# Attention of the second and third token block in chunks of 64 tokens, all eight heads at once, on quarters of the array

## The chip, the cores and the metric

The kernel runs on one core of a Trainium2 chip. Its time is the device time of one execution in microseconds (us). The engines are TensorE (PE, with its weight loads as PEld), VectorE (DVE), ScalarE (ACT), GpSimd (POOL) and SyncE (SP), which issues the DMAs.

## What is computed

Decayed linear attention over 2 x 8 heads, 768 tokens and a head dimension of 64, then two MLPs (512 to 2048 to 512) over the 1536 tokens. The attention goes over blocks of tokens with a state of 64 x 64 for each head:

```python
intra = np.einsum('bhic,bhjc->bhij', qb, kb) * Dmask[None]
intra = np.einsum('bhij,bhjd->bhid', intra, vb)
inter = np.einsum('bhid,bhde->bhie', qb * lam_pow[None], kv_state)
out[:, :, sl] = intra + inter
kv_state = lam_block[None, :, None, None] * kv_state + np.einsum('bhsd,bhse->bhde', kb_dec, vb)
...
x = _moe_ref(x=x, **moe_kwargs)
return _moe2_ref(x=x, **moe2_kwargs)
```

The length of a chunk is free, since any split of the tokens gives the same result.

## The kernel before, in words

The tokens are in three blocks of 512 (T). The first MLP runs block by block, each in 16 steps f (128 of the 2048 hidden features), then the second MLP over all blocks. A step is 12 matmuls into `h` (`mlp_h`) and, two steps later, 12 into `y` (`mlp_y`), each with 512 columns (`mm3`, lines 313 to 316: three single-pass matmuls stand for one of full precision, with high and low parts of weights and inputs). VectorE and ScalarE also turn the raw weights into these parts (`make_w1_ops`, lines 113 to 129) and apply the nonlinearity (lines 336 to 343).

Attention works in chunks of 128 tokens (C) and in two groups g of four heads, so each block has eight pairs (chunk, group). The eight of the first block run at the start (lines 494 to 525). Those of the second and third block are woven into the MLP steps of the block before: `att_visit` (line 537) runs at steps 0, 2, 4, ... 14 and 15 of the first block's MLP and at 2, 4, ... 14 and 15 of the second's, 17 visits (line 587). A visit issues the scores of the next pair (`att_s`, line 198) and the rest of the pair before (`att_av`): the values (line 238), the part from the state (line 244, not for the first chunk of a batch) and the update of the state (line 251, not for the last). Each is four matmuls in float32. The scores take 64 rows of the array and all its columns; two heads lie in the two row halves and write two PSUM banks. The other three take all rows and 64 columns, so two heads lie in the two column halves. All but the update stream 128 columns; the update streams 64.

After the visit ScalarE scales the state (line 256), copies the output (line 269) and scales the keys (line 208), GpSimd scales the queries (line 217), and VectorE adds the update to the state in two halves (line 284) and multiplies the scores by the mask in two halves (line 223). All orders are written out by hand, that of each engine and that of the DMA queue on SP. A pair's load is two DMAs of 256 KB in rows of 2 KB (line 173), with two buffers for each.

## Time and profile before

| what | us |
|---|---|
| median of three runs (594.11 to 595.8) | 595.7 |
| the profiled execution | 594.52 |
| its span, first to last instruction | 592.7 |
| TensorE busy in the span | 579.5 |
| VectorE busy in the span | 474.6 |

Busy time counts records, and matmuls overlap, so a busy TensorE can still run with more or less in it. A row of the timeline gives the start, the length and the number of instructions that were merged; the number of partitions x elements follows. `pa_s` are the PSUM tiles of the visits, `pa` and `att` those of the first block's attention. A matmul in float32 shows as two records, one of the MLP as one.

### The profile page before, as it was taken

The page shows a single profiled execution, that of the slowest core. Times are in us where ns is not written, and L with a number is a line of the kernel's source. Part 1 is how long each engine was busy: PE and PEld are TensorE (multiplying, and loading weights), DVE is VectorE, ACT ScalarE, POOL GpSimd, SP SyncE. Part 2 cuts the span into 40 slices and gives each one's busy share as a digit, 9 for nine tenths or more (in the row PEclk, how much of TensorE's full clock was granted, in tenths as well). Part 3 has the DMA queues.
Part 4 walks back from the last instruction along what each step waited for, and adds up shares of the span by engine and source line. Part 5 has one row for each costly group of instructions (what it writes and reads, how often), then busy time and mean ns, then how long its engine had stood idle before and what let it go on. Part 6 is the DMA issues. An engine that isn't in the chain of part 4 may idle for free.

```text
span 592.7 us, 8157 instructions
## 1 busy us (share of the span) xinstructions
PE 579.5 (98%) x3038; PEld 475.8 (80%) x3038; DVE 474.6 (80%) x772; ACT 352.4 (59%) x647; POOL 21.8 (4%) x37
## 2 busy tenths in 40 slices
PE   8878999999999999999999999999999999999997
PEld 7766888888888887888888888888888888888885
DVE  5999998975577653487798999988799888798882
ACT  3464456565434434555558887666777666866762
POOL 5200000000000000000000000000000000000000
PEclk9988999999999999999999999999999999999999
DMA  8954552556367532334443430000210000100001
GB/s 297 401 191 153 203 194 88 186 190 195 107 196 229 162 125 71 143 126 173 134 156 92 131 116 0 1 0 1 103 40 1 1 0 1 71 1 0 2 0 72
DMA packets 25961, 64.49 MB, mean 109 GB/s; under 512 B 2882, under 2 KB 2882, under 8 KB 25922
## 3 DMA queue, kind: packets, MB, share of 16 engines
q1 hardware_dynamic: 25922, 63.98, 31.8%
q8 instruction: 24, 0.39, 0.3%
q14 instruction: 15, 0.12, 0.1%
HBM read 53.48 MB, written 10.49 MB: 108 GB/s over the span
## 4 chain that ended last, share of the span: by engine, by line
PE 94%; DVE 5%; issue 1%; ACT 0%; DVEq 0%
PE y L314 15%; PE y L315 14%; PE y L316 14%; PE h L316 14%; PE h L315 14%; PE h L314 14%; PE pa_s L198 2%; PE pa_s L238 1%; DVE w L129 1%; PE pa L198 1%; DVE w L76 1%; PE pa_s L244 1%; DVE w L73 1%; PE pa L238 1%; DVE w L70 1%; PE pa L462 1%
## 5 line engine op out<-in xcount | busy, mean ns | idle before, releaser
L314 PE MATMUL h<-xlo,w 128*128 128x512 f32 x384 | 151.0, 393 | 5.6 <-DVE b L338 3.0
L316 PE MATMUL h<-xhi,w 128*128 128x512 f32 x384 | 150.9, 393 | 1.1 <-DVE w L129 1.1
L314 PE MATMUL y<-glo,w 128*128 128x512 f32 x384 | 151.3, 394 | 0.0
L315 PE MATMUL h<-xhi,w 128*128 128x512 f32 x384 | 150.6, 392 | 0.0
L316 PE MATMUL y<-ghi,w 128*128 128x512 f32 x384 | 149.6, 389 | 0.0
L315 PE MATMUL y<-ghi,w 128*128 128x512 f32 x384 | 149.5, 389 | 0.0
L314 PEld LDWEIGHTS h<-xlo,w 128*128 128x128 f32 x384 | 72.8, 190 | 21.8 <-DVE b L338 3.4
L316 PEld LDWEIGHTS h<-xhi,w 128*128 128x128 f32 x384 | 72.9, 190 | 17.2 <-DVE w L129 2.0
L314 PEld LDWEIGHTS y<-glo,w 128*128 128x128 f32 x384 | 72.0, 188 | 16.1 <-issue 0.7
L315 PEld LDWEIGHTS h<-xhi,w 128*128 128x128 f32 x384 | 72.8, 189 | 15.0
L316 PEld LDWEIGHTS y<-ghi,w 128*128 128x128 f32 x384 | 72.1, 188 | 15.2
L315 PEld LDWEIGHTS y<-ghi,w 128*128 128x128 f32 x384 | 72.1, 188 | 14.5
L349 ACT ACTIVATE a<-h,babs 128x512 f32<-128x512 f32 x48 | 33.0, 687 | 61.9 <-PE h L316 61.8
L340 ACT ACTIVATE ghi<-b 128x512 fp32r<-128x512 f32 x48 | 30.0, 628 | 43.7 <-DVE b L338 43.6
L336 ACT ACTIVATE a<-h 128x512 f32<-128x512 f32 x48 | 28.4, 592 | 39.9 <-PE h L316 39.7
L353 DVE SCALAR_TENSOR_TENSOR b<-b,babs,a 128x512 f32<-128x512 f32 x48 | 36.0, 750 | 19.6 <-ACT b L350 19.6
L341 DVE TENSOR_TENSOR glo<-b,ghi 128x512 fp32r<-128x512 f32 x48 | 33.5, 699 | 16.1 <-ACT ghi L340 13.9
L338 DVE SCALAR_TENSOR_TENSOR b<-a,h 128x512 f32<-128x512 f32 x48 | 32.7, 681 | 10.3 <-ACT a L337 7.0
L128 ACT ACTIVATE w<-w 128x512 fp32r<-128x512 f32 (+1 forms) x23 | 18.4, 800 | 36.7 <-DVE w L76 34.2
L351 ACT ACTIVATE p<-h,cab 128x512 f32<-128x512 f32 x48 | 37.6, 784 | 0.0
L355 ACT ACTIVATE a<-b,one 128x512 f32<-128x512 f32 x48 | 34.9, 728 | 3.4 <-DVE b L353 2.9
L357 DVE SCALAR_TENSOR_TENSOR p<-p,cab,h 128x512 f32<-128x512 f32 x48 | 35.8, 745 | 1.2
(75 smaller groups left out, 699.0 us busy)
## 6 DMA issues: line engine op xcount, KB each, us to landing
raw<-w_in SPq DMA_DIRECT2D x46, 512.0 KB, 3.8
raw<-w_in SPq DMA_DIRECT2D x9, 1024.0 KB, 4.9
att<-qkv_in SPq DMA_DIRECT2D x16, 256.0 KB, 5.4
qk<-qkv_in SPq DMA_DIRECT2D x16, 256.0 KB, 4.6
kv<-qkv_in SPq DMA_DIRECT2D x16, 256.0 KB, 3.3
w2d<-wp SPq DMA_DIRECT2D x16, 256.0 KB, 4.2
w<-w2d SPq DMA_DIRECT2D x16, 256.0 KB, 2.7
x2d<-o SPq DMA_DIRECT2D x12, 256.0 KB, 2.2
```

What stands on the lines that cost most here:

```text
L314: nc.tensor.matmul(acc, lhsT=wh, rhs=xl, start=first, stop=False)
L315: nc.tensor.matmul(acc, lhsT=wh, rhs=xh, start=False, stop=False)
L316: nc.tensor.matmul(acc, lhsT=wl, rhs=xh, start=False, stop=last)
L336: lambda: nc.scalar.activation(out=a, in_=h, func=AF.Relu, scale=-1.0),
L338: lambda: nc.vector.scalar_tensor_tensor(out=b, in0=a, scalar=-1.0, in1=h, op0=ALU.add, op1=ALU.max),
L340: lambda: nc.scalar.activation(out=ghi, in_=b, func=AF.Copy),
L341: lambda: nc.vector.tensor_tensor(out=glo, in0=b, in1=ghi.bitcast(F32), op=ALU.subtract)]
L349: nc.scalar.activation(out=a, in_=h, func=AF.Abs, scale=babs[:, 0:1])
L351: nc.scalar.activation(out=p, in_=h, func=AF.Identity, scale=cab[:, 3:4], bias=cab[:, 2:3])
L353: nc.vector.scalar_tensor_tensor(out=b, in0=b, scalar=babs[:, 1:2], in1=a, op0=ALU.mult, op1=ALU.add)
L355: nc.scalar.activation(out=a, in_=b, func=AF.Ln, bias=one[:, 0:1])
L357: nc.vector.scalar_tensor_tensor(out=p, in0=p, scalar=cab[:, 1:2], in1=h, op0=ALU.add, op1=ALU.mult)
```

## The change

In the second and third block a chunk is 64 tokens and holds all eight heads, which makes 16 chunks in place of 16 pairs. There are again 17 visits, at steps 2, 4, ... 12, 13, 14, 15 and at 2, 4, ... 14, 15. All four kinds of matmul now have 64 rows, 64 columns of the array and 64 columns streamed. There are eight of each kind in a visit. The scores of the next chunk are issued in turn with the values of the last one, and the updates with the state parts, so that four following matmuls address the four quarters of the array. The mask of two heads is put one below the other by a GpSimd copy. VectorE multiplies the scores in one instruction and adds the state in one; ScalarE scales the state in four. The first block keeps its chunks of 128, but its last chunk adds the old state to the update on TensorE, by an identity, and leaves it in the new layout. A chunk's load is eight DMAs of 64 KB in pieces of 256 bytes, with three buffers. The first is issued behind the weights of step 3, two more at steps 0 and 1, and the others behind the visits from step 4 on.

```diff
     def att_kq(c, g):
         qk, kv, kq = group[c, g][0], att_tile(c, g, 1), att_tile(c, g, 3)
-        if c % CB < CB - 1:
-            for a in range(2):
-                for h2 in range(2):
-                    r, h = slice(h2 * D, (h2 + 1) * D), 4 * g + 2 * a + h2
-                    if c >= NC:
-                        nc.scalar.activation(out=kq[:, 0, a, r], in_=kv[:, a, 0, r], func=AF.Copy,
-                                             scale=dmask[:, h, C - 1:C])
-            if c < NC:
-                nc.gpsimd.tensor_tensor(
-                    out=kq[:, 0].rearrange("p a (h d) -> p a h d", h=2),
-                    in0=kv[:, :, 0].rearrange("p a (h d) -> p a h d", h=2),
-                    in1=dmask[:, 4 * g:4 * g + 4, C - 1:C].rearrange("p (a h) i -> p a h i", h=2)
-                    .to_broadcast([P, 2, 2, D]), op=ALU.mult)
-        if c % CB:
+        nc.gpsimd.tensor_tensor(
+            out=kq[:, 0].rearrange("p a (h d) -> p a h d", h=2),
+            in0=kv[:, :, 0].rearrange("p a (h d) -> p a h d", h=2),
+            in1=dmask[:, 4 * g:4 * g + 4, C - 1:C].rearrange("p (a h) i -> p a h i", h=2)
+            .to_broadcast([P, 2, 2, D]), op=ALU.mult)
+        if c:
             nc.gpsimd.tensor_tensor(out=kq[:, 1], in0=qk[:, :, 0], in1=qpow[:, 2 * g:2 * g + 2],
...
@@ -244,47 +224,140 @@
                     nc.tensor.matmul(ps[0][r, 2 + a], lhsT=state[:, 2 * g + a, h2],
                                      rhs=kq[:, 1, a], start=False, stop=True,
                                      skip_group_check=True)
-        if not last:
+        for a in range(2):
+            for h2 in range(2):
+                r = slice(h2 * D, (h2 + 1) * D)
+                ro = slice((1 - h2) * D, (2 - h2) * D) if last else r
+                nc.tensor.matmul(pu[ro, a], lhsT=kq[:, 0, a, r], rhs=kv[:, a, 1, r],
+                                 start=a == 0 or not last, stop=not last, skip_group_check=True)
...
+        if last:
+            low()
             for a in range(2):
                 for h2 in range(2):
-                    r = slice(h2 * D, (h2 + 1) * D)
...
+                    ro = slice((1 - h2) * D, (2 - h2) * D)
+                    nc.tensor.matmul(pu[ro, a], lhsT=ident, rhs=state[:, 2 * g + a, h2],
+                                     start=False, stop=True, skip_group_check=True)
+            nc.scalar.activation(out=state[:, gs_, 0], in_=pu, func=AF.Copy)
+            return
...
+    CS = D
+    KB = CB * C // CS
+    ROWS = [slice(0, D), slice(D, P)]
+    chunk = {}
+    aa_tiles = []
+    def sm_load(k):
+        c, b = k // 2, k % 2
+        qk = qq.tile([P, NP, 2, CS], F32, tag="qk", name=f"qk{k}")
+        kv = qq.tile([P, NP, 2, D], F32, tag="kv", name=f"kv{k}")
+        chunk[k] = {"qk": qk, "kv": kv}
+        row = 4 * P
+        feat, nat = qkv[c, 0, 0], qkv[c, 0, 1]
+        step = C + (CS if b == 0 else -CS)
+        for rho, r in enumerate(ROWS):
+            for g in range(NP // 2):
+                nc.sync.dma_start(out=qk[r, 2 * g:2 * g + 2], in_=bass.AP(
+                    feat.tensor, feat.offset + (g * 2 * P + (1 - rho) * D) * row + b * CS,
+                    [[row, D], [2 * C, 2], [step, 2], [1, CS]]))
+                nc.sync.dma_start(out=kv[r, 2 * g:2 * g + 2], in_=bass.AP(
+                    nat.tensor, nat.offset + (g * 2 * P + (1 - b) * CS) * row + (1 - rho) * D,
+                    [[row, CS], [P, 4], [1, D]]))
+    def sm_products(n, d):
+        if not aa_tiles:
+            aa_tiles.extend(pa.tile([P, T], F32, tag=f"pa{i}", name=f"aa{i}")
+                            .rearrange("p (x m i) -> p x m i", x=2, m=NP) for i in range(2))
+            for r in ROWS:
+                nc.tensor.matmul(aa_tiles[1][r, 1], lhsT=pick[r], rhs=mask64[r, :, 1:CS + 1],
+                                 start=True, stop=True, skip_group_check=True)
+            nc.scalar.activation(out=qpow[:, :, 0:CS], in_=aa_tiles[1][:, 1], func=AF.Copy)
+        pn, pd = chunk.get(n), chunk.get(d)
+        for m in range(NP):
+            if pn:
+                for r in ROWS:
+                    nc.tensor.matmul(aa_tiles[0][r, 0, m], lhsT=pn["qk"][r, m, 1],
+                                     rhs=pn["qk"][r, m, 0], start=True, stop=True,
+                                     skip_group_check=True)
+            if pd:
+                for i, r in enumerate(ROWS):
+                    nc.tensor.matmul(aa_tiles[1][ROWS[1 - i], 0, m], lhsT=pd["kv"][r, m, 1],
+                                     rhs=pd["s"][r, m], start=m == 0, stop=d % KB == 0,
+                                     skip_group_check=True)
+        for m in range(NP):
+            if pd and d % KB < KB - 1:
+                for r in ROWS:
+                    nc.tensor.matmul(aa_tiles[0][r, 1, m], lhsT=pd["kv"][r, m, 0],
+                                     rhs=pd["kv"][r, m, 1], start=True, stop=True,
+                                     skip_group_check=True)
+            if pd and d % KB:
+                for i, r in enumerate(ROWS):
+                    nc.tensor.matmul(aa_tiles[1][ROWS[1 - i], 0, m], lhsT=state[r, m, 0],
+                                     rhs=pd["qk"][r, m, 0], start=False, stop=True,
+                                     skip_group_check=True)
+    def sm_decay(n):
+        qk, kv = chunk[n]["qk"], chunk[n]["kv"]
+        if n % KB < KB - 1:
+            for m in range(NP):
+                nc.scalar.activation(out=kv[:, m, 0], in_=kv[:, m, 0], func=AF.Copy,
+                                     scale=mask64[:, m, CS - 1:CS])
+        if n % KB:
+            nc.gpsimd.tensor_tensor(out=qk[:, :, 0], in0=qk[:, :, 0], in1=qpow[:, :, 0:CS],
+                                    op=ALU.mult)
+    def sm_mask(n):
+        b = chunk[n]
+        b["s"] = s = ap_.tile([P, NP, CS], F32, tag="s", name=f"s{n}")
+        nc.vector.tensor_tensor(out=s, in0=aa_tiles[0][:, 0], in1=mask64[:, :, 0:CS], op=ALU.mult)
+    def sm_out(d):
+        t, js = d * CS // T, slice(d * CS % T, d * CS % T + CS)
+        if t not in xraw:
+            xraw[t] = xr.tile([P, NP, T], F32, tag="xr", name=f"xr{t}")
+        first, last = d % KB == 0, d % KB == KB - 1
+        if not (first or last):
+            for m in range(NP):
+                nc.scalar.activation(out=state[:, m, 0], in_=state[:, m, 0], func=AF.Copy,
+                                     scale=qpow[:, m, CS - 1:CS])
+        nc.scalar.activation(out=xraw[t][:, :, js], in_=aa_tiles[1][:, 0], func=AF.Copy)
+        if first:
+            nc.scalar.activation(out=state[:, :, 0], in_=aa_tiles[0][:, 1], func=AF.Copy)
+        elif not last:
+            nc.vector.tensor_tensor(out=state[:, :, 0], in0=aa_tiles[0][:, 1],
+                                    in1=state[:, :, 0], op=ALU.add)
...
-        qq = actx.enter_context(tc.tile_pool(name="qq", bufs=2))
+        qq = actx.enter_context(tc.tile_pool(name="qq", bufs=3))
...
+        diag = ws.tile([P, DM], F32, tag="w", name="diag")[:, 0:C + 1]
+        tabs = ac.tile([P, 2, D], F32, name="tabs")
+        pick, ident = tabs[:, 0], tabs[:, 1]
...
+        for last in (D - 1, P - 1):
+            nc.gpsimd.affine_select(out=pick, in_=pick, pattern=[[0, D]], base=-last,
+                                    channel_multiplier=1, compare_op=ALU.not_equal, fill=1.0)
+            nc.gpsimd.affine_select(out=ident, in_=ident, pattern=[[-1, D]], base=D - 1 - last,
+                                    channel_multiplier=1, compare_op=ALU.not_equal, fill=1.0)
...
+        mask64 = dmask.rearrange("p (m h) i -> p m h i", h=2)[:, :, 1, CS:]
...
-        todo = atts[PB:]
+        todo = list(range(T // CS, NB * T // CS))
...
             load_whole(3)
+            sm_load(loads.pop(0))
...
             att_av(*atts[6])
             att_av(*atts[7])
+            nc.gpsimd.tensor_copy(
+                out=mask64[ROWS[1]],
+                in_=dmask.rearrange("p (m h) i -> p m h i", h=2)[ROWS[1], :, 0, 0:CS + 1])
...
         def att_visit(due, more):
             n = todo.pop(0) if more and todo else None
-            if n:
-                att_s(*n, aa)
-            if due:
-                att_av(*due.pop())
-                if loads:
-                    att_load(*loads.pop(0))
-            if n:
-                att_kq(*n)
-                att_mask(*n)
+            d = due.pop() if due else None
+            sm_products(n, d)
+            if d is not None:
+                sm_out(d)
+                del chunk[d]
+            if n is not None:
+                sm_decay(n)
+                sm_mask(n)
                 due.append(n)
...
+            visits = [(2, 4, 6, 8, 10, 12, 13, 14, 15), (2, 4, 6, 8, 10, 12, 14, 15)]
...
-                if f % 2 == 0 and (t == 0 or f) or f == NF - 1:
+                if f in visits[t]:
                     att_visit(due, t == 0 or f < NF - 1)
...
+                if loads and (f in visits[t][1 - t:] or t == 0 and f < 2):
+                    sm_load(loads.pop(0))
```

## Rows read from the trace of the kernel before

**Rows 1.** The page: the span, and busy time, share and instructions of two engines.

```profile
span 592.7 us, 8157 instructions
...
PE 579.5 (98%) x3038; PEld 475.8 (80%) x3038; DVE 474.6 (80%) x772; ACT 352.4 (59%) x647; POOL 21.8 (4%) x37
```
**Rows 2.** The page: the chain that ended last, its shares of the span by engine.

```profile
PE 94%; DVE 5%; issue 1%; ACT 0%; DVEq 0%
```
**Rows 3.** Stretches: length, busy us (instructions) of PE, PEld, DVE, ACT, POOL, granted clock, DMA.

```profile
30.00:52.00 22.00, 16.48 (x86) 12.41 (x86) 21.70 (x34) 13.48 (x28) 0.74 (x1) 0.91 0.43 154
...
52.00:60.00 8.00, 8.00 (x52) 6.35 (x53) 7.97 (x11) 3.59 (x7) 0.81 (x1) 0.82 0.65 241
...
130.00:240.00 110.00, 110.00 (x648) 89.68 (x647) 65.54 (x121) 48.15 (x104) 5.20 (x7) 1.00 0.47 149
```
**Rows 4.** Waits of TensorE: who for whom, us, times, longest.

```profile
PE h L314 <- DVE b L338: 3.0, 1, 3.0
...
PE h L314 <- ACT w L128: 1.4, 1, 1.4
...
PE h L316 <- DVE w L129: 1.1, 1, 1.1
```
**Rows 5.** Timeline of TensorE: start, us, line, operation, shape, count; two MLP steps, a visit, the next.

```profile
60.51 0.39 PE L314 MATMUL h<-xlo,w 128*128 128x512 f32 x1
...
65.95 0.39 PE L314 MATMUL h<-xlo,w 128*128 128x512 f32 x1
...
158.54 0.72 PE L198 MATMUL pa_s<-qk 64*128 64x128 f32 x8
...
160.11 0.40 PE L251 MATMUL pa_s<-kv,kq 128*64 128x64 f32 x8
...
171.56 0.71 PE L198 MATMUL pa_s<-qk 64*128 64x128 f32 x8
```
**Rows 6.** Timeline of TensorE: starts of four visits.

```profile
68.76 0.71 PE L198 MATMUL pa_s<-qk 64*128 64x128 f32 x8
...
81.54 0.71 PE L198 MATMUL pa_s<-qk 64*128 64x128 f32 x8
...
94.32 0.71 PE L198 MATMUL pa_s<-qk 64*128 64x128 f32 x8
...
106.89 0.71 PE L198 MATMUL pa_s<-qk 64*128 64x128 f32 x8
```
**Rows 7.** Timeline of TensorE: MLP matmuls around the first and the last visit.

```profile
26.41 0.39 PE L316 MATMUL h<-xhi,w 128*128 128x512 f32 x1
...
27.72 0.40 PE L315 MATMUL h<-xhi,w 128*128 128x512 f32 x1
...
230.69 0.39 PE L316 MATMUL h<-xhi,w 128*128 128x512 f32 x1
...
232.37 0.40 PE L315 MATMUL y<-ghi,w 128*128 128x512 f32 x1
```
**Rows 8.** Timeline of TensorE in the first block's last chunk.

```profile
20.83 0.28 PE L251 MATMUL pa<-att 128*64 128x64 f32 x2
...
20.94 0.27 PE L244 MATMUL pa<-att,state 128*64 128x128 f32 x1
...
20.95 0.32 PE L251 MATMUL pa<-att 128*64 128x64 f32 x3
```
**Rows 9.** Timeline of VectorE: state adds of the first block, masks of the first visit.

```profile
23.65 0.60 DVE L284 TENSOR_TENSOR state<-pa,state 64x128 f32<-64x128 f32 x2
...
29.88 0.76 DVE L223 TENSOR_TENSOR s<-pa_s,dmask 128x256 f32<-128x256 f32 x2
```
**Rows 10.** The page: the DMA queue: packets, MB, share of 16 engines.

```profile
q1 hardware_dynamic: 25922, 63.98, 31.8%
```
**Rows 11.** DMA from 20.3 to 20.8 us.

```profile
DMA packets 172, 0.20 MB, mean 397 GB/s; under 512 B 91, under 2 KB 91, under 8 KB 172
...
q1 hardware_dynamic: 172, 0.20, 114.7%
```

More of the change, by code (lines that the diff above doesn't have):

```diff
@@ L230, in att_av @@
         kv, s, kq, ps = b[1], b[2], b[3], b["ps"]
-        first, last = c % CB == 0, c % CB == CB - 1
+        first, last = c == 0, c == NC - 1
         pu = ps[1][:, 2].rearrange("p (a e) -> p a e", a=2)
@@ new lines, in att_av, with low @@
+        hi, lo = xg[0, 0, g]
+        gs_ = slice(2 * g, 2 * g + 2)
+        if not first:
+            for a in range(2):
+                nc.scalar.activation(out=state[:, 2 * g + a], in_=state[:, 2 * g + a],
+                                     func=AF.Copy, scale=qpow[:, 2 * g + a, C - 1:C])
+        nc.scalar.activation(out=hi[:, :, js], in_=ps[0][:, 2:4], func=AF.Copy)
+        def low():
+            nc.vector.tensor_tensor(out=lo[:, :, js], in0=ps[0][:, 2:4],
+                                    in1=hi[:, :, js].bitcast(F32), op=ALU.subtract)
@@ L248, in att_av @@
+        if last:
+            low()
             for a in range(2):
                 for h2 in range(2):
-                    r = slice(h2 * D, (h2 + 1) * D)
-                    nc.tensor.matmul(pu[r, a], lhsT=kq[:, 0, a, r], rhs=kv[:, a, 1, r],
-                                     start=True, stop=True, skip_group_check=True)
-        with tc.high_priority(HP):
-            if not (first or last):
-                for a in range(2):
-                    nc.scalar.activation(out=state[:, 2 * g + a], in_=state[:, 2 * g + a],
-                                         func=AF.Copy, scale=qpow[:, 2 * g + a, C - 1:C])
-            t, j = c // NC, c % NC
-            js = slice(j * C, (j + 1) * C)
-            if t == 0:
-                if j == 0:
-                    x_tiles(0, 0, g)
-                hi, lo = xg[0, 0, g]
-                nc.scalar.activation(out=hi[:, :, js], in_=ps[0][:, 2:4], func=AF.Copy)
-            else:
-                if (t, g) not in xraw:
-                    xraw[t, g] = xr.tile([P, 2, T], F32, tag=f"xr{g}", name=f"xr{t}_{g}")
-                nc.scalar.activation(out=xraw[t, g][:, :, js], in_=ps[0][:, 2:4], func=AF.Copy)
-            gs_ = slice(2 * g, 2 * g + 2)
-            def low():
-                if t == 0:
-                    nc.vector.tensor_tensor(out=lo[:, :, js], in0=ps[0][:, 2:4],
-                                            in1=hi[:, :, js].bitcast(F32), op=ALU.subtract)
-            if c == NC - 1:
-                low()
-            for h2 in range(2):
-                r = slice(h2 * D, (h2 + 1) * D)
-                if first:
-                    nc.scalar.activation(out=state[r, gs_, h2, :], in_=pu[r], func=AF.Copy)
-                elif not last:
-                    nc.vector.tensor_tensor(out=state[r, gs_, h2, :], in0=pu[r],
-                                            in1=state[r, gs_, h2, :], op=ALU.add)
-            if c < NC - 1:
-                low()
@@ new lines, in att_av @@
+                    ro = slice((1 - h2) * D, (2 - h2) * D)
[3 more added lines that the diff above has]
+            return
+        for h2 in range(2):
+            r = slice(h2 * D, (h2 + 1) * D)
+            if first:
+                nc.scalar.activation(out=state[r, gs_, h2, :], in_=pu[r], func=AF.Copy)
+            else:
+                nc.vector.tensor_tensor(out=state[r, gs_, h2, :], in0=pu[r],
+                                        in1=state[r, gs_, h2, :], op=ALU.add)
@@ L407, in fused_kernel @@
     nc.vector.memset(one, 1.0 + 1e-6)
-    atts = [(c, g) for c in range(NB * NC) for g in range(NP // 2)]
-    PB = NC * NP // 2
+    atts = [(c, g) for c in range(NC) for g in range(NP // 2)]
+    PB = len(atts)
     with ExitStack() as actx:
```

41 lines of the change are left out of this document (15 added, 26 removed).

## The prediction

> **What bounds the kernel now.** I read the page first: TensorE is busy for 579.5 of 592.7 us [rows 1] and holds 94% of the chain that ended last [rows 2]. The table by stretch says where that is not the whole truth. From 52 us on TensorE is never idle, and from 130 to 240 us, where half of the attention visits lie, VectorE is busy for only 65.5 of 110 us [rows 3]. So there a visit costs what its matmuls cost. From 30 to 52 us it is the other way round: VectorE is busy for 21.70 of 22.00 us, TensorE for 16.48 [rows 3], and the waits name the stops: 3.0 us for VectorE's b of the MLP, then 1.4 and 1.1 us for a weight tile that ScalarE and VectorE still make [rows 4]. What the change does to the kernel before 52 us is therefore read on VectorE, and after it on TensorE. The half clock after those stops (a mean of 0.82 of full speed from 52 to 60 us [rows 3]) costs 8 x 0.18 = 1.4 us.
>
> **A visit today, on TensorE.** One MLP step without a visit takes 65.95 - 60.51 = 5.44 us for its 24 matmuls [rows 5], so 0.227 each. Two steps are 10.88, and what is left between two visits two steps apart is a visit:
> - scores, value, state and update parts: 171.56 - 158.54 - 10.88 = 2.14 us [rows 5];
> - without update: 81.54 - 68.76 - 10.88 = 1.90; without state: 106.89 - 94.32 - 10.88 = 1.69 [rows 6];
> - scores alone: 27.72 - 26.41 less two MLP matmuls = 0.86; the last one, value and state: 232.37 - 230.69 less two = 1.23 [rows 7].
>
> Each of the four parts is four matmuls and shows as eight records, since a float32 matmul is two records. The state part costs 2.14 - 1.69 = 0.45, the update 0.24. The latter streams 64 columns and the former 128, and each addresses two column halves of the array, so eight records are four rounds of two: 0.11 us a round of 128 columns, 0.06 a round of 64. Scores alone are four rounds of 0.11, so 0.42 of the 0.86 is the way into the other shape and back; the last visit gives 1.23 - 8 x 0.11 = 0.35. I take 0.40.
>
> **Do tiles of the array run beside each other?** Between 20 and 22 us one sees it: update records start (20.83, 20.95) before the last state record of the same chunk does (20.94), so each half follows its own stream, and starts of 0.01 us apart occur [rows 8]. There the two streams share their rows and write different partitions of one bank. In today's scores the two streams lie in different rows and write different banks. Nothing shows four at once.
>
> **A visit after.** Per m the first loop issues two score and two value matmuls, which lie in four different quarters, and the second loop two update and two state matmuls, again in four. All stream 64 columns. That is 32 matmuls, 64 records, 16 rounds of four if all quarters run. A round of 64 columns is 0.06 us, so 0.96, and one way in and out instead of today's two changes of shape and more: 0.96 + 0.40 = 1.36 us. Chunks without update or state leave two quarters idle but need the same rounds.
> The cost of a round is the unknown: 0.055 if nothing is lost beside streaming, 0.12 if only two of four run. I take 0.06, the row with the same columns.
>
> **The sum after 52 us.** Before: nine visits of 2.14, three of 1.90, two of 1.69 and the last of 1.23, together 29.6 us. After: sixteen of 1.36, 21.8. Gain 7.8 us.
>
> **The sum before 52 us,** on VectorE. The last chunk of the first block no longer adds the state there: two pairs of adds like the one in [rows 9], 0.60 each. TensorE adds it with an identity instead, sixteen records (eight rounds, 0.5 us) behind ScalarE's two scalings of the state. By my estimate TensorE reaches the MLP some 0.5 us later by that (its eight rounds), which its 3.0 us stop swallows. Behind that wait stand the second group's value matmuls, and behind those the second group's split on VectorE; as that now comes later, I book 0.85 of the 1.2 us. The visit at step 0 goes, with its two masks (0.76 with the overlap to the next instruction [rows 9]; I take 0.7). The visit at step 2 keeps a single mask over 256 columns (half of that pair) and loses one pair of adds: 0.7 + 0.6 - 0.35, 0.9. VectorE reaches 52 us 0.85 + 0.7 + 0.9 = 2.4 us earlier, and TensorE with it. Lower bound 0, if another wait fills it; upper 2.4 + 1.4, if the half clock goes with the stops.
>
> **What costs nothing, and what covers it.** ScalarE scales the state in four pieces, not two, and copies two small states in the first block: under 1 us a visit on an engine that is idle for 62 of the 110 us [rows 3]. GpSimd gets three more selects, one larger memset and a copy of the masks, which waits for the last mask of the first block; behind it on GpSimd stands only the query product of the first visit. That visit, now at step 2, has scores alone and two extra matmuls (256 columns, 0.4 us), in the stretch where TensorE waits anyway. The visit that step 0 loses is made up at step 13, counted above. The first load moves behind the weights of step 3 on SP, and those come earlier by 1 MB of loads. A chunk's load is eight DMAs now, where a group's was two; SP waits before each for the visit that frees the buffer, and what stands behind it is the step's raw weights, needed a step later. Each load is issued two visits ahead, some 24 us, or 13 where steps 12 to 15 have a visit each.
> In pieces of 256 bytes a chunk is 2048 packets, 128 on each of 16 engines. A packet today takes 0.318 x 592.7 x 16 / 25922 = 0.116 us for a mean of 2.5 KB [rows 10]. Bounds for 256 bytes: by bytes 0.012, as a whole packet 0.116, so 1.5 to 14.8 us a chunk. In the half microsecond with the small table load, 172 packets took 1.147 x 0.5 x 16 = 9.2 us, and the 81 that were not small already make 9.4 at 0.116 [rows 11]: small ones cost next to nothing. I take 0.02, 2.6 us a chunk, well inside 13.
>
> **Sum:** 7.8 + 2.4 = 10.2 us. The profiled execution took 594.5 (span 592.7 and 1.8 around it), so it would take 584.3; the median shown, 595.7, is 1.2 above it, so 585.5.
>
> **Rivals.**
> Two at a time (slower, 10%). The two score matmuls of an m lie in different rows and write halves of one bank, as the two value matmuls do; today different rows go to different banks, so no row excludes that one bank takes one row group at a time. Then 16 rounds are 32: 1.92 + 0.40 = 2.32, sixteen are 37.1, 7.5 more than today, less 2.4: 600.8. It turns slower from a round of four at 0.10 us. For it: nothing but that the trace never shows the case. Against: streams that share rows, and streams that share columns, both run side by side today.
> Beside it: the Trainium skill, TensorEngine Tiling (Array Packing), section Restrictions and Gotchas, says that different row tiles cannot access the same PSUM bank simultaneously; by that rule the sum would be this rival's. No row here shows it either way.
> Records come too slowly (10%). The quickest today is two records in 0.06 us, 0.030 each. If the sequencer gave no more, the visit would again be 1.92 + 0.40; but a visit's first records wait in the queue behind MLP matmuls, so half of it is nearer: 1.44 + 0.40, sixteen are 29.4, no gain there, 593.3 in all.
> Beside it, the Trainium skill, TensorE: Matmul & The Clock Gate, section Part 1, has a floor of about 25 ns from start to start; the starts 10 ns apart in rows 8 speak against it as a floor between tiles.
> VectorE takes over (part of the forecast's range). From 52 to 60 us it is still busy for 7.97 of 8.00 us [rows 3]. The visits at steps 6 and 8 get 1.90 - 1.36 = 0.54 us shorter on TensorE but not on VectorE, where a wider add takes the place of a mask. If nothing is in hand there, that 1.1 us is waited for, and 1.4 if the clock falls again: 588.
> Loads late (3%): at 0.116 us a packet they would need 16 x 14.8 us beside transfers that fill half of the stretch, far over 600.
>
> **Numbers.** Forecast 72%, its own range 582.8 (early part 3.8, rounds of 0.055) to 590.4 (no early part, rounds of 0.07). Slow records 10%, two at a time 10%, late loads 3%, the remaining 5% small losses in several places. The range 581 to 593.5 holds the forecast and most of the slow records. A measurement tells 0.3%, 1.8 us, from no change: faster 80% (forecast, most of the slow records, part of the small losses), within it 7%, slower 13%.
>
> **What would show it.** Right: a full visit leaves about 1.36 us between MLP steps, its records come in fours at 0.06 us, the MLP's second stop ends near 49.4 instead of 51.8, and TensorE has no idle from there to 240. Wrong: records of a visit in pairs at 0.06; a wait of the score or value matmuls on the loads or on the mask; new stops between 52 and 80 us.

## The result and the profile after

The changed kernel took 588.81 us in the median of four runs (588.33 to 589.5), the kernel before on the same chip 594.9 (594.06 to 595.8): a ratio of 0.9898, with a 95% interval of 0.9876 to 0.992. It is faster by 1.0%; 585.5 was forecast, in a range of 581 to 593.5. The profiled execution took 588.79 us where that of before took 594.52, so 5.7 us are to be found in the two traces, and 10.2 were forecast. (The median of before ahead of the prediction, 595.7, was of three runs; with a fourth it is 594.9.)

The page of the changed kernel, the lines that answer to [rows 1, 2, 10]:

```profile
span 587.0 us, 9366 instructions
...
q1 hardware_dynamic: 52034, 63.98, 35.5%
...
PE 85%; DVE 8%; DMA 3%; ACT 2%; issue 2%; SPq 0%; DVEq 0%; ACTq 0%
```

TensorE is still the engine of the chain, with 85% for 94%, but 3% of the chain are now DMA, which held none before. The same bytes go in twice as many packets.

Its stretches, beside [rows 3]:

```profile
30.00:52.00 22.00, 17.47 (x83) 13.02 (x81) 21.66 (x32) 12.09 (x22) 1.25 (x1) 0.92 0.75 210
52.00:60.00 8.00, 8.00 (x87) 6.36 (x88) 8.00 (x11) 4.88 (x13) 0.96 (x1) 0.79 0.52 194
...
130.00:240.00 110.00, 108.86 (x915) 88.63 (x913) 64.03 (x109) 53.83 (x128) 5.63 (x7) 1.00 0.54 156
```

From 30 to 52 us VectorE is still busy for all but a third of a microsecond. From 130 to 240 us TensorE now has 1.14 us of idle time where it had none.

Its waits of TensorE, beside [rows 4]:

```profile
PE h L387 <- DVE b L411: 3.2, 2, 2.0
PE h L387 <- ACT w L128: 1.4, 1, 1.4
...
PE aa L309 <- DMA qk<-qkv_in: 0.7, 2, 0.5
```

The first stop of the MLP has become shorter, 2.0 us for 3.0. New are two waits of the scores for a load (line 309), and a second wait for VectorE's b, of 1.1 us.

The timeline of TensorE in the changed kernel: the first matmul of the MLP, the ends of the first and the last of its early stops, and the last matmul ahead of the visit at step 4 (start, length, line, shape, count, and in brackets the idle time ahead and what ended it):

```profile
26.43 0.50 PE L387 MATMUL h<-xlo,w 128*128 128x512 f32 x1
...
34.68 0.67 PE L387 MATMUL h<-xlo,w 128*128 128x512 f32 x1 [2.04 <-DVE b L411]
...
51.95 0.79 PE L389 MATMUL h<-xhi,w 128*128 128x512 f32 x1 [1.11 <-DVE w L129]
...
55.67 0.39 PE L389 MATMUL h<-xhi,w 128*128 128x512 f32 x1
```

And of the kernel before:

```profile
23.78 0.50 PE L314 MATMUL h<-xlo,w 128*128 128x512 f32 x1 [1.24 <-DVE xlo L274]
...
33.67 0.50 PE L314 MATMUL h<-xlo,w 128*128 128x512 f32 x1 [3.00 <-DVE b L338]
...
51.82 0.80 PE L316 MATMUL h<-xhi,w 128*128 128x512 f32 x1 [1.11 <-DVE w L129]
...
55.43 0.40 PE L316 MATMUL h<-xhi,w 128*128 128x512 f32 x1
```

Read these two as three distances. The MLP begins 2.65 us later (26.43 against 23.78). From there to the end of the first stop it is 8.25 us for 9.89, so 1.64 gained, and from there to the end of the last stop 17.27 for 18.15, so 0.88 gained. Together the last stop ends 0.13 us later than before, and the matmul ahead of the visit at step 4 starts 0.24 us later (55.67 against 55.43).

A visit, the same view of the changed kernel. The row at 39.70 is the first visit (scores alone), that from 55.98 to 57.08 a full one at step 4, and 68.18 the start of the next:

```profile
39.70 0.63 PE L309 MATMUL aa<-qk 64*64 64x64 f32 x16
...
55.98 0.27 PE L309 MATMUL aa<-qk 64*64 64x64 f32 x2
56.00 0.27 PE L314 MATMUL aa<-s,kv 64*64 64x64 f32 x2
56.09 0.23 PE L309 MATMUL aa<-qk 64*64 64x64 f32 x2
56.10 0.23 PE L314 MATMUL aa<-s,kv 64*64 64x64 f32 x2
56.15 0.23 PE L309 MATMUL aa<-qk 64*64 64x64 f32 x2
...
56.50 0.23 PE L320 MATMUL aa<-kv 64*64 64x64 f32 x2
56.51 0.22 PE L325 MATMUL aa<-qk,state 64*64 64x64 f32 x2
...
57.08 0.50 PE L387 MATMUL y<-glo,w 128*128 128x512 f32 x1
...
68.18 0.27 PE L309 MATMUL aa<-qk 64*64 64x64 f32 x2
```

Four records start within 0.02 us of one another. The next four follow the first after 0.11 us, and from then on a round of four comes every 0.06 us (56.09, 56.15): all quarters of the array run. The visit costs 68.18 - 55.98 - 10.88 = 1.32 us. From the start of the last matmul ahead of it (55.67, above) to the first behind it (57.08) it is 1.41 us, which is the handy measure for single visits.

The accounts then close. Sixteen visits of 1.32 are 21.1 us where they were 29.6, so -8.5; three waits after 100 us, told below, give back 3.0; the stretch up to the visit at step 4 gives +0.2. From the start of the last matmul (582.95 against 588.26) to the end of the span it is 4.1 us for 4.5, so -0.4, whose cause was not followed. That makes -5.7, as measured.

### The profile page after: what moved, and what is told of

It is laid out like the page before. It is cut to its first block, busy times and chain, and to the rows that moved or that the text cites. A ratio compares the mean times of both kernels' runs of the same rounds, so it can differ in the third digit from the quotient of the medians.

```text
span 587.0 us, 9366 instructions
## 1 busy us (share of the span) xinstructions
PE 574.5 (98%) x3570; PEld 472.1 (80%) x3570; DVE 469.0 (80%) x745; ACT 359.4 (61%) x687; POOL 25.5 (4%) x42
## 3 DMA queue, kind: packets, MB, share of 16 engines
q1 hardware_dynamic: 52034, 63.98, 35.5%
## 4 chain that ended last, share of the span: by engine, by line
PE 85%; DVE 8%; DMA 3%; ACT 2%; issue 2%; SPq 0%; DVEq 0%; ACTq 0%
PE y L387 13%; PE y L388 13%; PE y L389 13%; PE h L389 13%; PE h L387 13%; PE h L388 13%; DVE w L73 2%; DVE w L76 2%; DMA raw<-w_in 2%; PE pa L186 1%; DVE w L129 1%; PE aa L309 1%; DVE w L70 1%; PE pa L218 1%; DMA w2d<-wp 1%
## 5 line engine op out<-in xcount | busy, mean ns | idle before, releaser
L426 DVE SCALAR_TENSOR_TENSOR b<-b,babs,a 128x512 f32<-128x512 f32 x48 | 36.0, 750 | 21.0 <-ACT b L423 20.8
L414 DVE TENSOR_TENSOR glo<-b,ghi 128x512 fp32r<-128x512 f32 x48 | 34.8, 726 | 16.1 <-ACT ghi L413 14.6
```

The costliest lines, as they stand in the source:

```text
L414: lambda: nc.vector.tensor_tensor(out=glo, in0=b, in1=ghi.bitcast(F32), op=ALU.subtract)]
L426: nc.vector.scalar_tensor_tensor(out=b, in0=b, scalar=babs[:, 1:2], in1=a, op0=ALU.mult, op1=ALU.add)
```

## Where the other time went

**Loads.** Two visits late in the first block's MLP, and a stop in the second block, from the same timeline:

```profile
117.97 0.39 PE L389 MATMUL h<-xhi,w 128*128 128x512 f32 x1
...
119.42 0.27 PE L309 MATMUL aa<-qk 64*64 64x64 f32 x1 [0.53 <-DMA qk<-qkv_in]
...
120.27 0.50 PE L387 MATMUL y<-glo,w 128*128 128x512 f32 x1
...
125.61 0.39 PE L389 MATMUL h<-xhi,w 128*128 128x512 f32 x1
...
127.69 0.50 PE L387 MATMUL y<-glo,w 128*128 128x512 f32 x1
...
177.80 0.39 PE L389 MATMUL y<-ghi,w 128*128 128x512 f32 x1
179.33 0.50 PE L387 MATMUL h<-xlo,w 128*128 128x512 f32 x1 [1.14 <-DVE b L411]
```

The two visits leave 2.30 and 2.08 us in place of 1.41, 0.89 and 0.67 too many. At the stop, 177.80 to 179.33 is 1.53 us, and the matmul behind follows after 0.34; two steps from matmul to matmul are otherwise 0.46, so with the restart the idle 1.14 costs 1.4. Together that is 3.0 us. What SP did before is in its own timeline, of the changed kernel:

```profile
97.38 0.61 SPq L289 DMA_DIRECT2D qk<-qkv_in  x1
...
102.71 9.14 SPq L100 DMA_DIRECT2D raw<-w_in  x4
111.95 0.54 SPq L289 DMA_DIRECT2D qk<-qkv_in  x1
...
117.58 0.60 SPq L292 DMA_DIRECT2D kv<-qkv_in  x1
```

An issue with 256 pieces takes some 0.6 us on SP, so a chunk's eight take 5.3 us from one start to the next free slot (97.38 to 102.71); a load of before took 0.33 to 0.42 for 128 rows. Behind one chunk four issues of raw weights took 9.14 us, where such an issue alone takes 0.3 to 0.5; SP waits there for buffers that are not free. That wait is not new (four such issues took 8.43 and 8.28 us at 98 and 111 us in the kernel before); the eight long issues around it are. So the next chunk's first issue came at 111.95 and its last at 117.58, 0.7 us before the visit that wanted it (118.29). The chain into the stop at 179 goes back through VectorE to a store of weights to DRAM, which took 4.35 us and which SP issued at 164.27, behind eight loads of a chunk (157.70 to 163.58):

```profile
164.27 4.35 DMA w2d<-wp
```

The transfers were not the trouble: the packets doubled, but their time rose only from 31.8% to 35.5% of the span.

**The start.** The beginning of TensorE's work in the changed kernel, and then in the kernel before:

```profile
7.44 1.97 PE L528 MATMUL pa<-dmask,tabs 64*64 64x128 f32 x16 [0.60 <-DVE att L203]
9.35 2.08 PE L186 MATMUL pa<-att 64*128 64x128 f32 x16
```

```profile
7.45 1.09 PE L450 MATMUL pa<-dmask,diag 128*64 128x128 f32 x16 [0.60 <-DVE att L223]
8.47 1.25 PE L198 MATMUL pa<-att 64*128 64x128 f32 x16
```

The scores in the second rows are the same work, and take 2.08 us for 1.25. TensorE is still at its lower level (1.2 GHz) here, and is at 2.4 GHz in the kernel before. The granted clock of the stretches shows 1.00 here in both kernels, since the trace's records of it only begin with the step to the full level, at 7.17 us in the kernel before and at 14.36 in the changed one. I call that moment the rise. The spacing of the score records agrees: a pair follows the last every 0.21 us ahead of it and every 0.11 behind it. VectorE has to wait for these scores; the groups of VectorE up to 26 us (line, shape, count, busy us and mean ns, idle before and its releasers), of the changed kernel and of the kernel before:

```profile
L203 DVE TENSOR_TENSOR att<-pa,dmask 128x256 f32<-128x256 f32 x16 | 5.9, 417 | 3.6 <-PE pa L186 3.4
```

```profile
L223 DVE TENSOR_TENSOR att<-pa,dmask 128x256 f32<-128x256 f32 x16 | 5.9, 416 | 1.8 <-PE pa L198 1.7
```

It waits 3.4 us for the scores where it waited 1.7. One difference ahead of it is `make_qpow`: its 16 records (eight matmuls, line 528) now use 64 rows of the array where they used 128 (`pick[ROWS[1]]`).

## The experiments

Twelve runs were made, in three groups (e1 to e4, e5 to e8, e9 to e12). Those of a group shared one chip and the runs of the kernel before there (median 595.39 us in the first group, 595.06 in the second, 595.11 in the third).

**e1_qpow_full_rows**: the powers made with all 128 rows again, the rest as changed.

```diff
+        pick1 = diag[:, 2 * C:2 * C + D]
+        nc.gpsimd.memset(pick1, 0.0)
+        nc.gpsimd.affine_select(out=pick1, in_=pick1, pattern=[[0, D]], base=1 - C,
+                                channel_multiplier=1, compare_op=ALU.not_equal, fill=1.0)
...
-                    nc.tensor.matmul(ps[r, a], lhsT=pick[ROWS[1]],
-                                     rhs=dmask[ROWS[1], 4 * g + 2 * a + h2, 1:C + 1],
+                    nc.tensor.matmul(ps[r, a], lhsT=pick1,
+                                     rhs=dmask[:, 4 * g + 2 * a + h2, 1:C + 1],
```

> The matmuls that pick the decay powers (line 528) take all 128 rows again, as before the change, instead of 64. Theory A: in the changed kernel these sixteen records of 64x64 are why TensorE stays at the half clock until 14.4 us instead of 7.2 us; then it is at full clock by about 7.2 to 8 us here, the first MLP matmul starts near 24.3 us instead of 26.9, the second stop of the MLP ends near 49.5 instead of 51.95, and the kernel takes about 586.3 (2.4 less than the changed kernel). Theory B: the clock rises when it happens to, whatever these matmuls are; then it comes at either time, and the time goes with it. Theory C: the early gain is lost to the wait of TensorE for ScalarE in the last chunk of the first block; then the clock may rise earlier, but the second stop still ends near 51.9 and the time stays at 588.8.

Measured: 586.44 us (585.97 to 587.74, five runs), ratio 0.9859 (0.9835 to 0.9884). The rise came at 8.93 us, the first matmul of the MLP at 24.32 and the end of the last early stop at 49.85, near the 49.4 of the forecast, and the time is that of theory A. (The 26.9 us of the expectation for the changed kernel should be 26.43.) The edit is not quite pure, since it adds a memset and a select on GpSimd. The load waits stayed.

**e2_loads_first**: a chunk's load issued ahead of the step's raw weights.

```diff
                     att_visit(due, t == 0 or f < NF - 1)
+                if loads and (f in visits[t][1 - t:] or t == 0 and f < 2):
+                    sm_load(loads.pop(0))
                 for w in now:
...
-                if loads and (f in visits[t][1 - t:] or t == 0 and f < 2):
-                    sm_load(loads.pop(0))
```

> In each step the eight DMAs of a chunk are issued ahead of the step's raw weights instead of behind them. Theory A: the score matmuls at steps 14 and 15 of the first block wait (0.9 and 0.7 us) because SP first waits for VectorE to free the raw buffers (9 us before the load of 112 us) and then needs 0.65 us for each of the eight issues; then both waits are gone and the time is about 587.2 (1.6 less). Theory B: the packets of 256 bytes are what is late, since they share the DMA engines; then the waits stay. Rival on the other side: the raw weights now come 5 us later, VectorE waits for them, and the time is 589 to 591.

Measured: 591.1 us (588.23 to 592.14, six runs), ratio 0.9923 (0.9897 to 0.9949), so no gain on the changed kernel and by the medians a loss of 2.3 to 2.6 us, though the intervals overlap. Its waits of TensorE:

```profile
PE h L387 <- DVE xlo L57: 1.5, 1, 1.5
...
PE aa L309 <- DVE s L343: 0.8, 2, 0.4
```

No wait for a load is left. But now the raw weights come later, and VectorE, which takes them apart, is late with the masked scores and with the second block's inputs. SP's time is short for both; here the order only said who pays.

**e3_kinds_apart**: all scores, then all values, then all updates, then all state parts.

```diff
                                      skip_group_check=True)
+        for m in range(NP):
             if pd:
...
+        for m in range(NP):
             if pd and d % KB:
```

> In a visit all score matmuls come first, then all value ones, then the updates, then the state parts, so that four following matmuls lie in two quarters of the array, not four. Theory A: the gain of a visit comes from four quarters at once, and TensorE starts records of a far quarter only from nearby in the program; then a visit takes 32 rounds of 0.06 and 0.40, about 2.3 us instead of 1.32, sixteen of them cost 15.7 more, and the time is about 604. Theory B: each quarter has a deep stream of its own, so the order within a visit hardly matters; then the visit stays near 1.4 us and the time near 589.

Measured: 593.21 us in one run, and a visit of 80.90 - 68.26 - 10.88 = 1.76 us, between the two expectations. The timeline of TensorE shows why:

```profile
68.58 0.51 PE L309 MATMUL aa<-qk 64*64 64x64 f32 x10
68.87 0.27 PE L315 MATMUL aa<-s,kv 64*64 64x64 f32 x2
68.92 0.28 PE L309 MATMUL aa<-qk 64*64 64x64 f32 x3
```

The first value record starts when ten of the sixteen score records have; it runs beside the last six. So matmuls of idle quarters are drawn ahead of waiting ones, but only for about six records; at the two later changes of kind (69.16 and 69.46 us) ten of sixteen have started as well. Of the interleaving, the last three rounds of a kind are had in any order and the rest only by writing them in turn. Thirteen visits of the sixteen are full ones and cost 0.44 more, the one without update 0.3, the one without state 0.1, the last nothing, some 6.1 us in all. The waits for loads, met later now, shrank by 1.6 us (0.43 for 1.56 at steps 14 and 15, and 0.9 for 1.4 at the stop of the second block), which leaves 4.5; the kernel is 4.4 to 4.8 slower than the changed one.

**e4_changed_again**: the changed kernel, no edit, for a second trace beside the first three.

> The changed kernel once more, for one thing: when the clock rises in it. If it is set by the work, at 14.4 us again, and the first MLP matmul near 26.9 us; if it goes by chance, at another time, such as 7.2 to 11 us, and then the first MLP matmul starts up to 2.5 us earlier.

Measured: 588.36 us in one run. The rise came at 12.64 us, the first matmul of the MLP at 26.02. The visits at steps 14 and 15 left 3.10 and 2.44 us. TensorE stayed at full clock after the stops (1.00 from 52 to 60 us), where the first trace has a granted clock of 0.79:

```profile
51.55 0.50 PE L389 MATMUL h<-xhi,w 128*128 128x512 f32 x1 [1.11 <-DVE w L129]
...
53.72 0.39 PE L389 MATMUL h<-xhi,w 128*128 128x512 f32 x1
```

From the end of the last stop to the matmul ahead of the visit at step 4 this is 2.17 us for 3.72, so the half clock there costs 1.55. With the earlier rise this run is 1.95 us ahead at 53.72, and yet it ends only 0.4 earlier: the waits at steps 14 and 15 take back 1.2 (2.7 for 1.56) and the stop of the second block 0.3. As long as the loads are late, time gained on TensorE ahead of them is mostly waited away.

**e5_whole_rows**: the inputs of the second and third block are laid out so that a chunk's load is two DMAs of 256 KB in rows of 2 KB. Only the order of the numbers in `qkv_in` differs (it is laid out before the launch, as it was).

```diff
-        for rho, r in enumerate(ROWS):
-            for g in range(NP // 2):
-                nc.sync.dma_start(out=qk[r, 2 * g:2 * g + 2], in_=bass.AP(
...
+        nc.sync.dma_start(out=qk.rearrange("p m x i -> p (m x i)"), in_=qkv[c, b, 0])
+        nc.sync.dma_start(out=kv.rearrange("p m x e -> p (m x e)"), in_=qkv[c, b, 1])
```

> The host lays q, k and v of the second and third block out as the visits use them, so a chunk is loaded by two DMAs of 256 KB in rows of 2 KB instead of eight of 64 KB in pieces of 256 bytes. All else is the changed kernel. Theory A: eight issues of 0.65 us on SP a chunk are what makes the loads, the raw weights and the parked weights late; then the waits of the visits at steps 14 and 15 of the first block (0.9 and 0.7 us) and the stop near 178 us (1.1) go, and the time is about 586.2. Theory B: SP is held up by its waits for raw buffers, whatever the loads cost; then at least one of the waits at steps 14 and 15 stays, and the time is above 587.5.

Measured: 585.03 us (581.73 to 586.53, six runs), ratio 0.9821 (0.9795 to 0.9848). All visits leave 1.40 to 1.41 us, and the stop of the second block is gone, as theory A had it. Four issues of raw weights still take 9.93 us there (at 97.99), so it was the eight long issues that made the loads late. The profiled execution is the fastest of the six, 581.73; its rise came at 6.88 us, though its powers are made with 64 rows, and its clock did not fall after the stops:

```profile
23.90 0.49 PE L378 MATMUL h<-xlo,w 128*128 128x512 f32 x1
...
49.42 0.50 PE L380 MATMUL h<-xhi,w 128*128 128x512 f32 x1 [1.11 <-DVE w L129]
```

The 7.1 us to the profiled execution of the changed kernel (588.79) are then 2.5 from the rise (23.90 for 26.43), 1.55 from the clock after the stops and 3.0 from the loads. Of the six runs the two shortest, 581.73 and 583.84, have a mean granted clock of 1.00, the others 0.993 or 0.994.

**e6_rows_and_qpow**: the edits of the first and the fifth together.

> Both: the loads in whole rows and the decay powers picked with all 128 rows. If the two causes are separate their gains add: 588.8 - 2.4 - 2.6 = 583.8, close to the 585.5 and 584.3 that the prediction's sum gave for the change without them. If the clock or VectorE gives one of them back, 585 to 586.5.

Measured: 583.52 us (583.07 to 584.13, four runs), ratio 0.9801 (0.9781 to 0.9822): the lowest median, ahead of both kernels; ahead of the fifth by 1.5 us, with intervals that overlap, so the two are not told apart. Its rise came at 11.23 us, so even with 128 rows it can be late. From its waits of TensorE:

```profile
PE h L378 <- DVE b L402: 2.0, 1, 2.0
...
PE pa L524 <- POOL att L191: 0.9, 1, 0.9
```

The load waits and the stop of 1.1 us for b are gone. The last row is a wait ahead of the powers, which begin at 7.71 us; it is not the price of the select that was added, since in the fifth, without it, they begin at 7.72.

**e7_eight_issues_2KB**: the layout of the fifth, but eight DMAs of 64 KB again, each over 32 partitions.

```diff
+        for i in range(4):
+            r = slice(i * P // 4, (i + 1) * P // 4)
+            nc.sync.dma_start(out=qk[r].rearrange("p m x i -> p (m x i)"), in_=qkv[c, b, 0][r])
+            nc.sync.dma_start(out=kv[r].rearrange("p m x e -> p (m x e)"), in_=qkv[c, b, 1][r])
```

> As with whole rows, but each 256 KB is issued as four DMAs of 32 partitions, so a chunk is eight issues again, in packets of 2 KB. Theory A1: the number of issues is what costs; then SP spends about 5 us a chunk and the time is 588 to 589 as in the changed kernel. Theory A2: the number of pieces in an issue (256 against 32) sets its length; then an issue is about 0.35 us, a chunk 2.8 us, and the time is near that with two DMAs, within 1 us of 586.2.

Measured: 585.35 us (584.35 to 586.76, five runs), ratio 0.9836 (0.9813 to 0.9858). SP's timeline:

```profile
97.24 0.41 SPq L286 DMA_DIRECT2D qk<-qkv_in  x1
```

With the same eight issues, but 32 pieces of 2 KB in each, an issue takes some 0.4 us, and the median is within 0.3 us of the fifth's. A part of the trouble stays in the trace: the visits at steps 14 and 15 still leave 1.87 and 2.39 us, 1.4 too many, so the number of issues counts too. The stop of the second block is gone. What makes an issue long was not settled: the 256 pieces differ from these 32 in number, in size and in the shape of the access, and 128 rows of 2 KB took no longer (0.33 to 0.42) than 32.

**e8_two_buffers**: two buffers for the loads, and the load of step 1 left to the visit at step 4, so that each chunk is issued one visit later.

```diff
-        qq = actx.enter_context(tc.tile_pool(name="qq", bufs=3))
+        qq = actx.enter_context(tc.tile_pool(name="qq", bufs=2))
...
-                if loads and (f in visits[t][1 - t:] or t == 0 and f < 2):
+                if loads and (f in visits[t][1 - t:] or t == 0 and f < 1):
```

> The changed kernel with two buffers of loads instead of three; a chunk is issued one visit ahead instead of two. If the third buffer is what hides the loads, the visits at steps 12 to 15 of the first block, 6.7 us apart, wait for loads that need over 5 us of issue alone and stand behind raw weights: 5 to 15 us in sum, a time of 594 to 604. If it hides little, the time is within 2 us of 588.8.

Measured: 601.68 us in one run, slower than the kernel before. Its waits of TensorE are headed by

```profile
PE aa L309 <- DMA qk<-qkv_in: 10.2, 7, 4.5
```

and visits leave up to 8.35 us. Around two of the long waits TensorE fell to half clock, for 6.8 us each (a granted clock of 0.50 from 114.7 to 121.5 us and from 128.4 to 135.2), so such a wait is paid more than once. With two buffers the change is a loss.

**e9_before_half_rows**: in the kernel before, the powers alone made with 64 rows.

```diff
-                    nc.tensor.matmul(ps[r, a], lhsT=pick, rhs=dmask[:, 4 * g + 2 * a + h2, 1:C + 1],
+                    nc.tensor.matmul(ps[r, a], lhsT=pick[D:P],
+                                     rhs=dmask[D:P, 4 * g + 2 * a + h2, 1:C + 1],
```

> The kernel before, with one thing of the change: the sixteen records that pick the decay powers take 64 rows of the array instead of 128. Theory A (these matmuls delay the rise of the clock): the clock rises near 12 to 14 us in the profile instead of 7.2, and the time is 1 to 2.4 us above that of the kernel before in the same runs. Theory B (the clock rises by chance between some 7 and 14 us): no difference in time beyond 0.5 us, and the rise is anywhere in that stretch.

Measured: 596.1 us (594.33 to 597.55, twelve runs), ratio 1.002 (1.0006 to 1.0035): a loss of 1.0 us, less than half of the 2.4 that undoing it gave. In the profiled execution, the fastest of the twelve, the rise came at 6.84 us, ahead of the powers (7.44), so this trace says nothing of their effect.

**e10_qpow_again**: the first edit again, beside the changed kernel on one chip.

> The changed kernel with the powers picked by all 128 rows, again, on the same chip as the changed kernel itself. Theory A: 2.4 less than the changed kernel, and a rise near 9 us. Theory B: the medians are within 1 us of each other, and the rise may be as late as 14 us.

Measured: 586.28 us (585.45 to 587.62, five runs), ratio 0.985 (0.9828 to 0.9872); the rise at 6.34 us, the end of the last early stop at 49.99. Its first row of powers on TensorE's timeline, to compare with 1.97 us at 7.44 above:

```profile
7.33 1.09 PE L533 MATMUL pa<-dmask,diag 128*64 128x128 f32 x16 [0.67 <-DVE att L203]
```

**e11_changed_beside**: the changed kernel, no edit, for that comparison.

> The changed kernel on the same chip, as the measure for the one above: about 588.8 by the first runs. Theory A: a rise between 12 and 15 us. Theory B: a rise anywhere from 7 us on, and single times that spread by 2 us and more.

Measured: 588.49 us (587.04 to 589.36, six runs), ratio 0.9882 (0.9862 to 0.9902); the rise at 14.56 us, the end of the last early stop at 51.95. The edit is worth 2.2 us here, as it was 2.4 against the first runs of the changed kernel, with intervals that overlap a little.

**e12_before_beside**: the kernel before, no edit.

> The kernel before once more, for when its clock rises. Theory A: near 7 us again. Theory B: anywhere up to 14 us.

Measured: 595.25 us in one run; the rise at 8.52 us, the first matmul of the MLP at 24.04, the end of the last early stop at 52.41.

## Why the prediction was right, and where it was not

**The visit** was forecast at 1.36 us and took 1.32: sixteen rounds of four records at 0.06, and 0.4 around them. This is the step that carries the result, and both rivals about it fall.

Two at a time: the scores of the first visit show the disputed case alone, two row groups writing one bank. Their sixteen records at 39.70 take 0.63 us; less the last record's own 0.22 that is 0.41 for the seven steps between eight rounds of two. Had the bank taken one row group at a time, fifteen steps of 0.06 and the last record would be 1.1 us. The Trainium skill, TensorEngine Tiling (Array Packing), section Restrictions and Gotchas, would have given that; the measurement decides against it for row groups that write different partitions of the bank, as these do. The Trainium skill, PSUM — Partial Sum Buffer, section PSUM bank collisions raise a hardware error, quotes the same rule, but what it has as measured for two row groups is a collision in one bank and the same group of 32 partitions; the trace, with different partitions, fits that narrower reading.

Records too slow: 64 records start in some 0.94 us, so 15 ns each on average. The floor of 25 ns in the Trainium skill, TensorE: Matmul & The Clock Gate, section Part 1, does not bind between quarters; its Part 3 has about 4 ns between starts of different tiles, and the four starts within 0.02 us, some 7 ns apart, agree with that better.

**VectorE takes over** did not happen: from 52 to 60 us VectorE is busy for all of 8.00 us, but no wait of TensorE stands there.

**Rows 8** were read a little too far. Of the two update starts cited only 20.83 lies before 20.94, and the update writes another bank (`ps[1]`) than the state part (`ps[0]`). Nothing of the sum hangs on it.

**The early part** was forecast at 2.4 us and gave -0.13. Its own terms were right: 0.85 and 0.7 up to the first stop (1.64 measured from the MLP's start), 0.9 between the stops (0.88 measured). What failed is the clause that TensorE reaches the MLP "some 0.5 us later", which "its 3.0 us stop swallows". It came 2.65 us later; and the stop is set by VectorE, which had waited for the same late scores, so the stop could swallow only what VectorE did not lose itself. The sum took the clock at the start as in the kernel before and had no term for it. In e5, with an early rise, the early part comes out as forecast: the MLP begins at 23.90, 0.12 us after that of before, and the last stop ends at 49.42, for the 49.4 of the forecast; e7, with the same layout and a late rise, has 25.86 for the MLP. From the MLP's first matmul to the end of the last stop it is 25.5 us in the changed kernel with the late rise as with the early one.

The cause of the 2.65 is thus the clock at the start. Over all fourteen executions with a profile, the MLP's first matmul goes with the rise, from 23.7 to 24.5 us where it came before 9 us to 25.5 and more where it came after 11:

| kernel | rows of the powers | powers begin, us | rise, us | first matmul of the MLP, us |
|---|---|---|---|---|
| powers again (e10) | 128 | 7.33 | 6.34 | 24.46 |
| before, half rows (e9) | 64 | 7.44 | 6.84 | 23.69 |
| whole rows (e5) | 64 | 7.72 | 6.88 | 23.90 |
| before | 128 | 7.45 | 7.17 | 23.78 |
| before again (e12) | 128 | 7.45 | 8.52 | 24.04 |
| powers (e1) | 128 | 7.44 | 8.93 | 24.32 |
| rows and powers (e6) | 128 | 7.71 | 11.23 | 25.51 |
| eight issues (e7) | 64 | 7.45 | 12.31 | 25.86 |
| two buffers (e8) | 64 | 7.45 | 12.31 | 25.86 |
| changed again (e4) | 64 | 7.44 | 12.64 | 26.02 |
| kinds apart (e3) | 64 | 7.45 | 14.33 | 26.42 |
| changed | 64 | 7.44 | 14.36 | 26.43 |
| loads first (e2) | 64 | 7.45 | 14.44 | 26.43 |
| changed beside (e11) | 64 | 7.45 | 14.56 | 26.43 |

That is only partly the change's doing. In four executions, two with either number of rows, the rise came before the powers began, so their rows can have had no part in it. In the other ten the powers began at the lower level, and there the rise came at 8.5 to 11.2 us with 128 rows (three of three) and at 12.3 to 14.6 with 64 (seven of seven). So the rows of the powers go with how late a late rise is, and undoing the 64 rows gave 2.2 to 2.4 us; whether the rise comes before them at all looks like chance, and in the kernel before the same edit cost only 1.0. Why 64 rows should delay it was not settled. The Trainium skill, TensorE: Matmul & The Clock Gate, section Part 1, says that the number of slow matmuls at a kernel's start differs from run to run of one kernel. The rises between 12.64 and 14.56 us of the changed kernel agree.

**The half clock after the stops** was priced at 1.4 us, and e4 has 1.55 for it. It stayed in the changed kernel's first trace, and where it did not come (e4) the late loads took most of its gain.

**Loads late** stood at 3%, by a mechanism that is not the one that came. The packet price was right enough: I took 0.02 us for one of 256 bytes, and twice the packets raised the DMA's share by only 3.7 points. What I left out is SP's own time, 0.6 us an issue for 0.33 to 0.42, eight times a chunk, and that SP stands for 9 us before raw weights whose buffers are not free. "Well inside 13" compared the transfer of 2.6 us with 13, where 5.3 us of issue and 9 of waiting stand ahead of it. It cost 3.0 us by the trace; whole rows gave back 3.5 to 3.8 by the medians (588.49 and 588.81 to 585.03), in which the clock has a share.

**The forecast of 585.5** was 3.3 us too low: 2.6 from the early part and 3.0 from the loads against it, the visits 0.7 better than booked, 0.4 behind the last matmul that no term had, and the 1.2 added from the profiled execution to the median, which was not there afterwards (588.79 and 588.81). The main step was right in mechanism and size. That the time lies in the range owes something to the range, which is 12.5 us wide where the change is 6: two terms failed, and the whole gain is six tenths of the forecast one. With the loads in whole rows and the powers from 128 rows the kernel takes 583.52 (e6). Of what was to show it, the fours of records and the visit came; the last stop's end at 49.4 did not (51.95), nor a TensorE without idle time to 240 us.

## What to carry to other kernels

Small matmuls that lie in different quarters of the array run four at a time at the rate of one, if the program writes them in turn: each quarter looks ahead only a few records. When loads are cut into smaller pieces, count the time of the issuing engine, the issues by their length and its waits for other buffers, before that of the transfers; here a layout in memory that made long rows helped, and another order of the issues did not. Time that TensorE gains ahead of late loads is waited away there, so mend the loads first. When work is cut at the start of a kernel, look first at whether TensorE's clock rises as early as before, in the lengths of equal records, and compare single traces only after that.

## What was not expected of the hardware

- Two row groups wrote different partitions of one PSUM bank side by side: sixteen records in 0.63 us.
- The four quarters have streams of their own with a short look ahead: a kind of matmul for idle quarters started when six records of the kind before were still to start, at all three changes of kind in a visit (e3).
- An issue on SP took 0.33 to 0.42 us with 128 rows of 2 KB, some 0.4 with 32 of them (e7), and about 0.6 with 256 pieces of 256 bytes.
- The clock rose anywhere between 6.3 and 14.6 us after the start, in kernels that differ by a few matmuls; the 8 us between show as 2.7 us at the MLP's first matmul.
- The fall to half clock after the last stop cost 1.55 us where it came (3.72 for 2.17 us, changed kernel and e4), and came in some executions of one kernel and not in others.
